# Moving the 72-row loads of strided values forward on the load queue, in a fused sparse attention and feed-forward kernel

## The chip, the cores and the metric

The kernel runs on one core of a Trainium2 chip. The metric is the device time of one execution in microseconds (us). Before the change the median of three runs is 280.25 us (278.87 to 281.23).

## What is computed

Attention over 8 batches, 8 heads, 576 positions and a head size of 64 is followed by a product of four weight matrices. Heads 0 to 3 see a local window of 32 positions; heads 4 to 7 see the positions that are congruent to their own modulo 32 ("strided").

```python
mask_local = (rel >= 0) & (rel < 32)
mask_strided = (rel >= 0) & (pos[None, :] % 32 == pos[:, None] % 32)
attn = softmax(where(mask, q @ k.T / 8, -1e9))
x = (attn @ v).transpose(0, 2, 1, 3).reshape(4608, 512)
out = (((x @ w1) * (x @ w2)) @ w3) @ w_out
```

w1 and w2 are 512 x 1024, w3 is 1024 x 1024 and w_out is 1024 x 512. Inputs and output are float32.

## The kernel before, in words

**Stages.** The program is one long unrolled order of work. TensorE's order is written out by hand (`pe` keeps it as written); the other engines follow it. Batch 0's attention runs alone at the start, four pairs of heads p0 to p3 (p0 and p1 local, p2 and p3 strided). Then come the first products of x with w1 and w2 (`aps` L535, `bps` L544), then eight rounds that fold w3 and w_out into one matrix w34 (`fold_tr` transposes a block of w3, L627; `fold_mm` multiplies it, L585). Batch 1's attention is spread among these rounds and the first outputs by the list `plan`. From then on each token tile's products (L535, L544, L585) host the next batch's attention in their gaps.

**Loads.** All loads are issued by one queue, SP (SyncE), in the order in which the program names them. A load writes float32 into a tile of the pool `stgp` (nine buffers), and an engine, mostly POOL (GpSimd), casts it to float16. An issue on SP waits until its buffer is free. It also waits on one of eight semaphores that the loads use in turn: a load waits until the load eight places ahead of it has landed.

The calls that set the order of the loads, in batch 0 and for the weights and batch 1, are:

```python
    load_qk(0, 0, "pa")
    load_rest(0, "v")
    load_qk(0, 1)
    load_vL(0)
    load_vX(0)
    load_w12(0)
...
    for jc in range(1, 6):
        load_w3(jc, "p")
    load_qk(1, 0)
    load_w3(6, "p")
    load_rest(1)
    load_w3(7, "p")
    load_vL(1)
    load_qk(1, 1)
    load_vX(1)
```

`load_qk` is a pair of loads of q and k for four heads (L182). `load_rest` loads their last 64 positions (L192). `load_vL` (L198) brings the values of the local heads: four transfers of 96 rows (L204), with a POOL cast (L205) and a POOL copy (L88) for each two heads. `load_vX` (L208) brings the values of the strided heads: four transfers of 72 rows into `sy` (L213), two of 7 rows (L218) and four of 112 rows (L220) into `st`, then a cast of `sy` (L221) and one or two casts of `st` (L223) on POOL, all into `v16X`. `load_w12` brings w1 and w2 (L173), `load_w3` (L162) and `load_wo` (L157) the other weights.

**Who waits for them.** The local pairs multiply by `v16L` and the strided pairs by `v16X` (`ah_PV`, L468). The first product with w1, `aps` at L535, needs the first cast of w1 into `w1h`. `fold_tr` of block jc needs the cast of that block of w3.

Of the kernel before, what the change touches and what calls it, by code (L numbers as in the profile page):

```python
# [14 lines left out]
def _ap(t: bass.AP, off_add, dims):  # L15
    return bass.AP(tensor=t.tensor, offset=t.offset + off_add, ap=dims)
# [3 lines left out]
def kernel(  # L20
# [11 lines left out]
    nc = tc.nc  # L32
    B, H, S, D = q.shape
# [15 lines left out]
    XW, XN, YW = 126, 4, 72  # L49
# [19 lines left out]
    AHEAD = 2  # L69
# [7 lines left out]
    def behind(ins):  # L77
        return tc.issue_after(ins.ins) if ins is not None else nullcontext()
# [4 lines left out]
    def copy(eng, out, in_):  # L83
        if eng == "a":
            return nc.scalar.copy(out=out, in_=in_)  # L85
        elif eng == "v":
            return nc.vector.tensor_copy(out=out, in_=in_)  # L87
        return nc.gpsimd.tensor_copy(out=out, in_=in_)  # L88
# [23 lines left out]
    for i in range(1, LT):  # L112
# [5 lines left out]
                          in_=_ap(maskX, 0, [[maskX.ap[0][0], XW], [0, XN - 1], [1, XW]]))  # L118
# [7 lines left out]
    v16X = [consts.tile([XW, 4, XN + 1, D + 1], FP16, name=f"v16X{i}") for i in range(2)]  # L126
# [33 lines left out]
    def load_w3(jc, eng):  # L160
        st = stgp.tile([P, DF], FP32, tag="stg")
        nc.sync.dma_start(st, moe_w3[bass.ds(jc * P, P), :])  # L162
        t = ffn.tile([P, DF], FP16, tag="w3n", bufs=6)
        w3n[jc] = t
        copy(eng, t, st)
# [13 lines left out]
    def load_qk(b, grp, engs="pp"):  # L179
        for nm, ten, eng in (("q", q, engs[0]), ("k", k, engs[1])):  # L180
            st = stgp.tile([P, 4, 4, D], FP32, tag="stg")
            nc.sync.dma_start(st.rearrange("p h c d -> p h (c d)"),  # L182
                              ten[b, 4 * grp:4 * grp + 4, 0:NM].rearrange("h (p c) d -> p h (c d)", c=4))
            t = qkp.tile([P, 4, 4, D], FP16, tag=f"{nm}{grp}")
            with behind(setup["p"] if b == 0 and grp == 0 else None):
                copy(eng, t, st.rearrange("p h c d -> p c h d"))
            x16[(b, nm, grp)] = t

    def load_rest(b, eng="p"):
        st = stgp.tile([P, H, D], FP32, tag="stg")  # L190
        for i, ten in enumerate((q, k)):
            nc.sync.dma_start(st[64 * i:64 * i + 64], ten[b, :, NM:S].rearrange("h p d -> p h d"))  # L192
        t = qkp.tile([P, H, D], FP16, tag="r")
        with behind(setup["v"] if b == 0 else None):
            copy(eng, t, st)
        x16[(b, "r")] = t

    def load_vL(b, hps=(0, 1)):  # L198
        vt = v16L[b % 2]
        for hp in hps:  # L200
            hs = slice(2 * hp, 2 * hp + 2)
            st = stgp.tile([P, 2, LT, D], FP32, tag="stg")
            for h in range(2):
                nc.sync.dma_start(st[0:LQ, h], v[b, 2 * hp + h].rearrange("(t p) d -> p t d", p=LQ))  # L204
            nc.gpsimd.tensor_copy(out=vt[0:LQ, hs, :, 0:D], in_=st[0:LQ])  # L205
            copy("p", vt[LQ:P, hs, 0:LT - 1, 0:D], vt[0:32, hs, 1:LT, 0:D])

    def load_vX(b):  # L208
        vt = v16X[b % 2]
        sv = v[b, 4:8]  # L210
        sy = stgp.tile([YW, 4, D], FP32, tag="stg")
        for h in range(4):
            nc.sync.dma_start(sy[:, h], sv[h].rearrange("(t x) d -> t x d", x=32)[:, 28:32])  # L213
        st = stgp.tile([XW, 4, 4 * D], FP32, tag="stg")
        n0 = 16 * 7
        for t in range(2):
            r0 = n0 + 7 * t
            nc.sync.dma_start(st[r0:r0 + 7], sv[:, NM + 32 * t:NM + 32 * t + 28].rearrange("h (a c) d -> a h (c d)", c=4))  # L218
        for h in range(4):
            nc.sync.dma_start(st[0:n0, h], sv[h, 0:NM].rearrange("(t a c) d -> t a (c d)", a=8, c=4)[:, 0:7])  # L220
        nc.gpsimd.tensor_copy(out=vt[0:YW, :, XN, 0:D], in_=sy)  # L221
        for hs in ((slice(0, 2), slice(2, 4)) if b == 0 else (slice(0, 4),)):
            nc.gpsimd.tensor_copy(out=vt[:, hs, 0:XN, 0:D], in_=st[:, hs].rearrange("p h (c d) -> p h c d", c=4))  # L223


# [511 lines left out]
    for p, s in enumerate(pairs):  # L737
        b, i = divmod(p, 4)
# [33 lines left out]
    load_qk(0, 0, "pa")  # L772
    load_rest(0, "v")
    load_qk(0, 1)
    load_vL(0)
    load_vX(0)
    load_w12(0)
    load_w12(1)
# [3 lines left out]
    for jc in range(1, 6):  # L782
        load_w3(jc, "p")
    load_qk(1, 0)
    load_w3(6, "p")
    load_rest(1)
    load_w3(7, "p")
# [4 lines that stand above are left out]
    while pos[0] < batch_end[0]:  # L792
# [28 lines left out]
    load_vL(2)  # L821
    load_qk(2, 1)
    load_vX(2)
    over = over_parts()
    tile1 = ab_parts(1) + o_parts(1)
# [66 lines left out]
```

## Time and profile before

| | before |
|---|---|
| median of three runs | 280.25 us |
| profiled execution | 278.93 us |
| its span | 277.2 us |
| TensorE busy | 259.6 us |
| POOL busy | 98.6 us |
| mean granted TensorE clock | 0.98 |
| bytes moved by the loads' queue | 38.87 MB |

Times in the profile count from the start of the span. PE is TensorE's matmul, PEld its weight load, DVE is VectorE, ACT ScalarE, POOL GpSimd, SP SyncE; SPq is SP's own queue, whose rows are issues of transfers. A row of the timeline has the start, the length, the engine, the line, the operation, its tiles, the number of instructions merged in it, and in brackets the idle time ahead of it with what ended it. A row of the windows view has a stretch, its length, the busy time of PE, PEld, DVE, ACT and POOL (with instructions), the granted TensorE clock, the mean busy share of the 16 DMA engines and the GB/s that they moved. Shares can pass 1, since packets overlap.

### The profile page before, as it was taken

To read this page: it belongs to the slowest core of one execution; us is meant where nothing else is said; L and a number is where in the kernel's file an instruction comes from. 1 tells how busy PE (TensorE), PEld (TensorE's weight loads), DVE (VectorE), ACT (ScalarE), POOL (GpSimd) and SP (SyncE) were. 2 spreads that over 40 slices of the span, in tenths; PEclk is the share of its full clock that TensorE was granted. 3 is DMA by queue.
4 is the path that set the end of the run, shared out by engine and by line. 5 is a ranking of instruction groups with operands and counts; after the bars stand their busy time and mean duration, and the time that the engine had idled before them with its cause. 6 is when DMAs were issued, how large, how long until landed. Compare 5 with 4: busy or idle time off the path is not lost.

```text
span 277.2 us, 6384 instructions
## 1 busy us (share of the span) xinstructions
PE 259.6 (94%) x2474; PEld 138.8 (50%) x2474; DVE 146.6 (53%) x334; ACT 146.7 (53%) x310; POOL 98.6 (36%) x116
## 2 busy tenths in 40 slices
PE   2956999989989999999999999999999999999995
PEld 1743345645645555555555555555555544444442
DVE  6551343346777547854875577467547752320320
ACT  2750433475755665666665655665665664324322
POOL 3545677493554813646637258200000000000000
PEclk9975999999999999999999999999999999999999
DMA  7949999958979759969699598410030003003003
GB/s 210 223 145 365 398 399 371 193 176 244 252 229 254 199 180 258 225 187 322 197 248 277 168 255 204 148 73 4 0 116 38 2 38 116 0 6 146 1 10 142
DMA packets 61310, 48.65 MB, mean 176 GB/s; under 512 B 32032, under 2 KB 52704, under 8 KB 61280
## 3 DMA queue, kind: packets, MB, share of 16 engines
q1 hardware_dynamic: 56096, 38.87, 50.7%
q10 hardware_dynamic: 5184, 9.37, 8.9%
q8 instruction: 19, 0.31, 0.5%
q14 instruction: 11, 0.09, 0.1%
HBM read 38.80 MB, written 9.44 MB: 174 GB/s over the span
## 4 chain that ended last, share of the span: by engine, by line
PE 87%; ACT 4%; DMA 3%; DVE 2%; issue 1%; SPq 1%; POOL 0%; DVEq 0%; ACTq 0%
PE ops L585 25%; PE aps L535 23%; PE bps L544 22%; PE sps L335 3%; PE ps L487 3%; PE sps L301 2%; PE pt L258 2%; DMA st<-in_k_dram 2%; DMA st<-in_moe_w_dram 2%; PE tps L345 1%; PE trp L627 1%; PE pt L301 1%; PE sps L415 1%; ACT ptm L440 1%; ACT pte L453 1%
## 5 line engine op out<-in xcount | busy, mean ns | idle before, releaser
L535 PE MATMUL aps<-xT,w1h 128*128 128x512 f16 (+1 forms) x288 | 75.3, 383 | 3.9 <-POOL w1h L88 3.4
L544 PE MATMUL bps<-xT,w2h 128*128 128x512 f16 (+1 forms) x288 | 74.7, 376 | 0.0
L585 PE MATMUL ops<-w,abt 128*128 128x512 f16 x280 | 67.0, 379 | 0.2 <-ACT osb L596 0.2
L547 DVE TENSOR_TENSOR abt<-bps,asb 128x512 f16<-128x512 f32 (+1 forms) x72 | 48.7, 679 | 32.2 <-PE bps L544 29.8
L515 ACT COPY asb<-aps 128x512 f32<-128x512 f32 (+1 forms) x72 | 42.4, 593 | 43.1 <-PE aps L535 39.2
L88 POOL CAST t<-st 128x1024 f16<-128x1024 f32 (+1 forms) x46 | 46.6, 1018 | 28.0 <-DMA st<-in_q_dram 13.4
L535 PEld LDWEIGHTS <-w1h 128*128 128x128 f16 x288 | 26.7, 99 | 33.9 <-POOL w1h L88 3.6
L544 PEld LDWEIGHTS <-w2h 128*128 128x128 f16 x288 | 26.1, 98 | 26.4 <-issue 0.3
L585 PEld LDWEIGHTS <-abt 128*128 128x128 f16 x280 | 25.3, 98 | 26.2 <-issue 0.3
L326 ACT ACTIVATE pte<-sps 128x1024 f16<-128x1024 f32 (+1 forms) x24 | 24.6, 1026 | 11.4 <-PE sps L301 11.4
L596 ACT COPY osb<-ops 128x512 f32<-128x512 f32 x35 | 20.6, 589 | 17.4 <-PE ops L585 17.4
L495 ACT COPY xT<-ps 128x504 f16<-128x504 f16 x16 | 9.2, 578 | 27.0 <-PE ps L487 27.0
L479 DVE TENSOR_TENSOR xqs<-sps,rcp 128x768 f16<-128x768 f32 (+1 forms) x24 | 21.4, 891 | 0.8
L315 DVE TENSOR_TENSOR ptm<-pte,maskL 128x1152 f16<-128x1152 f16 (+2 forms) x16 | 12.6, 790 | 15.1 <-ACT pte L326 13.6
L315 DVE TENSOR_TENSOR ptm<-pte,maskX 126x1152 f16<-126x1152 f16 (+2 forms) x16 | 12.0, 754 | 15.5 <-ACT pte L326 13.4
L85 ACT COPY qT<-pt 128x224 f16<-128x224 f16 (+4 forms) x60 | 18.0, 361 | 3.1 <-ACT osb L596 1.9
L223 POOL CAST v16X<-st 126x1024 f16<-126x1024 f32 (+1 forms) x9 | 8.8, 975 | 28.8 <-DMA st<-in_v_dram 26.4
L205 POOL CAST v16L<-st 96x768 f16<-96x768 f32 x16 | 14.4, 899 | 8.3 <-DMA st<-in_v_dram 5.8
L585 PE MATMUL ops<-woh,w3T 128*128 128x512 f16 x64 | 15.6, 379 | 0.0
L487 PEld LDWEIGHTS <-xqs 126*128 126x128 f16 (+3 forms) x176 | 12.0, 100 | 7.2 <-DVE xqs L479 0.6
L87 DVE COPY kT<-pt 128x512 f16<-128x512 f16 (+4 forms) x48 | 14.1, 323 | 1.2 <-ACT qT L85 0.5
L487 PE MATMUL ps<-id,xqs 126*128 126x126 f16 (+3 forms) x176 | 14.4, 215 | 0.2 <-DVE xqs L479 0.2
(95 smaller groups left out, 248.3 us busy)
## 6 DMA issues: line engine op xcount, KB each, us to landing
out_dram<-osb ACTq DMA_DIRECT2D x35, 256.0 KB
st<-in_q_dram SPq DMA_DIRECT2D x16, 512.0 KB
st<-in_k_dram SPq DMA_DIRECT2D x16, 512.0 KB
st<-in_moe_w_dram SPq DMA_DIRECT2D x16, 512.0 KB
st<-in_v_dram SPq DMA_DIRECT2D x32, 144.0 KB
st<-in_v_dram SPq DMA_DIRECT2D x32, 112.0 KB
st<-in_moe_w_out_dram SPq DMA_DIRECT2D x4, 512.0 KB
st<-in_q_dram SPq DMA_DIRECT2D x8, 128.0 KB
```

What stands on the lines that cost most here:

```text
L85: return nc.scalar.copy(out=out, in_=in_)
L88: return nc.gpsimd.tensor_copy(out=out, in_=in_)
L315: nc.vector.tensor_mul(o.rearrange("p (a x) -> p a x", x=x), i.rearrange("p (a x) -> p a x", x=x), _ap(s.mask, lo, [[s.mask.ap[0][0], s.kr ...
L326: nc.scalar.activation(out=pv[0:kr, :, lo:hi], in_=src, func=AF.Exp, bias=0.0, scale=scale)
L479: nc.vector.tensor_mul(s.xqs[0:w, c0:c0 + l].rearrange("p i h d -> p h i d"), xv[:, :, :, 0:D], _ap(rcp, 0, [[rcp.ap[0][0], w], [LT, 2], [ ...
L487: pe(nc.tensor.transpose(ps[:, s.q[t]:s.q[t] + l], s.xqs[0:l, t].rearrange("p h d -> p (h d)"), id16[0:l, 0:l]))
L515: nc.scalar.copy(out=st["asb"][:, 0:nt], in_=st["a"][:, 0:nt])
L535: pe(nc.tensor.matmul(st["a"][:, 0:nt], w1h[:, ci, bass.ds(jc * P, P)], xT[ci][:, tok], start=(ci == 0), stop=(ci == KM - 1)))
L544: pe(nc.tensor.matmul(st["b"][:, 0:nt], w2h[:, ci, bass.ds(jc * P, P)], xT[ci][:, tok], start=(ci == 0), stop=(ci == KM - 1)))
L547: nc.vector.tensor_mul(abts[tch][:, jc, skip:], st["b"][:, 0:nt], st["asb"][:, 0:nt])
L585: pe(nc.tensor.matmul(st["ps"], lhs(ci), rhs(ci), start=(ci == 0), stop=(ci == KF - 1)))
L596: nc.scalar.copy(out=osb, in_=ps)
```

## The change

The four 72-row transfers and the cast of `sy` become a function of their own, `load_vX0`. For batch 0 it is called ahead of `load_vL(0)`, for batch 1 between `load_qk(1, 0)` and `load_w3(6)`. For the later batches `load_vX` calls it at its start, where the transfers stood. The cast of `st` is split in two for batch 1 as well as for batch 0. In the order of the built program the 182 instructions of SP are the same ones; POOL has one more; on DVE a reciprocal and a multiplication of pair p2 change places. The orders on PE and ACT are unchanged. Line numbers after the function grow by 5 (L218 and L220 by 6), and L213 becomes L212.

```diff
-    def load_vX(b):
-        vt = v16X[b % 2]
+    def load_vX0(b):
         sv = v[b, 4:8]
         sy = stgp.tile([YW, 4, D], FP32, tag="stg")
         for h in range(4):
             nc.sync.dma_start(sy[:, h], sv[h].rearrange("(t x) d -> t x d", x=32)[:, 28:32])
+        nc.gpsimd.tensor_copy(out=v16X[b % 2][0:YW, :, XN, 0:D], in_=sy)
+
+    def load_vX(b):
+        vt = v16X[b % 2]
+        sv = v[b, 4:8]
+        if b >= AHEAD:
+            load_vX0(b)
         st = stgp.tile([XW, 4, 4 * D], FP32, tag="stg")
...
-        nc.gpsimd.tensor_copy(out=vt[0:YW, :, XN, 0:D], in_=sy)
-        for hs in ((slice(0, 2), slice(2, 4)) if b == 0 else (slice(0, 4),)):
+        for hs in ((slice(0, 2), slice(2, 4)) if b < AHEAD else (slice(0, 4),)):
             nc.gpsimd.tensor_copy(out=vt[:, hs, 0:XN, 0:D], in_=st[:, hs].rearrange("p h (c d) -> p h c d", c=4))
...
     load_qk(0, 1)
+    load_vX0(0)
     load_vL(0)
     load_vX(0)
     load_w12(0)
...
     load_qk(1, 0)
+    load_vX0(1)
     load_w3(6, "p")
     load_rest(1)
     load_w3(7, "p")
```

AHEAD is 2.

## The prediction

> **What bounds the kernel now.** I read the page first (busy shares, the slices, the chain), then the chain in order of time, then the timelines of PE, SP and POOL over the first 24 us, then the windows.
>
> ```profile
> PEclk9975999999999999999999999999999999999999
> DMA  7949999958979759969699598410030003003003
> ...
> PE 87%; ACT 4%; DMA 3%; DVE 2%; issue 1%; SPq 1%; POOL 0%; DVEq 0%; ACTq 0%
> ```
>
> PE carries 87% of the chain, so only its holes can be shortened by moving loads. Nearly all the hole time lies in the first 24 us, where slices 3 and 4 also show a granted clock of 0.7 and 0.5. Slice 3 (13.9 to 20.8 us) has the DMA engines at 4 tenths, between fuller slices: something other than the DMA engines holds the loads there.
>
> The chain in order of time, and PE's own rows at that place:
>
> ```profile
> 17.55 4.77 DMA st<-in_moe_w_dram
> ...
> 22.37 1.05 POOL w1h L88
> ...
> 23.47 1.03 PE aps L535 x2
> ```
>
> ```profile
> 15.94 0.54 PE L468 MATMUL xpl<-v16L,ptm 128*128 128x65 f16 x12
> ...
> 18.82 0.76 PE L468 MATMUL xpl<-v16X,ptm 126*128 126x65 f16 x10 [2.08 <-POOL v16X L223]
> 19.39 0.68 PE L487 MATMUL ps<-id,xqs 128*128 128x128 f16 x6
> 23.47 1.03 PE L535 MATMUL aps<-xT,w1h 128*128 128x512 f16 x2 [3.40 <-POOL w1h L88]
> ```
>
> PE idles 2.08 us for the strided values and 3.40 us for the first cast of w1. From 23.47 on it is nearly full. The end is therefore set by when w1's first load is issued (17.55), and that by SP, whose rows follow end to end:
>
> ```profile
> 4.87 4.78 SPq L204 DMA_DIRECT2D st<-in_v_dram  x4
> 9.69 3.41 SPq L213 DMA_DIRECT2D sy<-in_v_dram  x4
> 13.14 0.81 SPq L218 DMA_DIRECT2D st<-in_v_dram  x2
> 14.00 3.43 SPq L220 DMA_DIRECT2D st<-in_v_dram  x4
> 17.55 4.66 SPq L173 DMA_DIRECT2D st<-in_moe_w_dram  x8
> ```
>
> ```profile
> 4.90:9.70 4.80, 3.77 (x30) 2.61 (x32) 3.02 (x10) 2.32 (x4) 1.50 (x2) 1.00 1.15 313
> 9.70:12.30 2.60, 2.59 (x43) 2.04 (x40) 0.91 (x4) 2.27 (x6) 1.74 (x3) 1.00 1.28 220
> 12.30:17.50 5.20, 4.11 (x71) 3.18 (x68) 3.55 (x12) 4.12 (x9) 3.19 (x5) 1.00 0.24 68
> 17.50:20.50 3.00, 1.25 (x16) 1.05 (x15) 1.25 (x5) 0.52 (x2) 1.23 (x2) 0.53 0.63 201
> 20.50:24.00 3.50, 0.53 (x2) 0.26 (x3) 0.13 (x1) 0.25 (x1) 1.39 (x2) 0.50 1.00 359
> 24.00:28.00 4.00, 4.00 (x23) 1.99 (x22) 1.33 (x5) 0.58 (x1) 2.77 (x3) 0.51 1.00 369
> ```
>
> The DMA engines are full to 12.3 us, at a share of 0.24 and 68 GB/s from 12.3 to 17.5, and full again from 20.5. In the middle stretch SP's issuing is the bound.
>
> The Trainium skill (DMA: Bandwidth & Descriptors, section Issuing engines are not separate DMA queues) says that the time to start a transfer is usually small beside the transfer. Here the trace differs: 0.24. By that rule the order of issue would be worth nothing and the sum would stay 280.25, which is the first rival's result.
>
> **The change, part by part.**
>
> *Batch 0, the 72-row transfers go ahead of the 96-row ones.* SP issues the same 18 transfers of q's rest to w1, so the question is whether the order changes what they cost. Single issues from the timeline of SP:
>
> ```profile
> 6.06 0.63 SPq L204 DMA_DIRECT2D st<-in_v_dram  x1
> ...
> 7.77 1.88 SPq L204 DMA_DIRECT2D st<-in_v_dram  x1
> ...
> 14.68 1.47 SPq L220 DMA_DIRECT2D st<-in_v_dram  x1
> ...
> 16.82 0.60 SPq L220 DMA_DIRECT2D st<-in_v_dram  x1
> ```
>
> A 96-row issue takes 0.63 us or 1.88 us; the long one falls while the DMA engines still drain q and k, so I read its excess of 1.25 us as SP held by a full queue. The small issues at 9.69 (0.85 each) bring little data, and are sent when the queue is about to run empty. After the change the four small ones are sent in the full stretch: 4.87 + 3.41 = 8.28. Then come the four 96-row ones. By the rule of the eight semaphores the third and the fourth wait for q's and k's second loads to land, which the casts show:
>
> ```profile
> 9.08 1.04 POOL L88 CAST t<-st 128x1024 f16<-128x1024 f32 x1 [3.30 <-DMA st<-in_q_dram]
> 10.63 1.04 POOL L88 CAST t<-st 128x1024 f16<-128x1024 f32 x1 [0.51 <-DMA st<-in_k_dram]
> 12.02 0.83 POOL L205 CAST v16L<-st 96x768 f16<-96x768 f32 x1 [0.35 <-DMA st<-in_v_dram]
> 12.91 0.71 POOL L88 COPY v16L<-v16L 32x640 f16<-32x640 f16 x1
> ...
> 15.35 0.40 POOL L221 CAST v16X<-sy 72x256 f16<-72x256 f32 x1
> 18.16 0.61 POOL L223 CAST v16X<-st 126x512 f16<-126x512 f32 x1 [2.41 <-issue]
> 19.46 0.62 POOL L223 CAST v16X<-st 126x512 f16<-126x512 f32 x1 [0.70 <-DMA st<-in_v_dram]
> ```
>
> So the fourth can't go before 10.6 us. It then takes 0.63 at least (11.25, against 13.14 before for the next issue: 1.9 us earlier) and 1.88 at most (12.5: 0.6 us earlier). If the excess returns in full and the first three also take their old times, nothing is gained; if the long 112-row issue (1.47, 0.87 over its neighbours) no longer meets what held it, 0.9 more is gained. Bounds: 0 and 2.8 us. I take 1.9, the row of 0.63 for the fourth, since the two loads ahead of it that filled the queue have landed by then.
>
> The 96-row loads are issued up to 3.41 us later. Their data lands when the DMA engines reach it, and these are full until 12.3 in either order, so the first cast (12.02) moves by about 0.5 us, bounded by 0 and 3.4. The product of p1 (15.94) then slips by as much. What hides it is PE's idle 2.08 + 3.40 = 5.5 us, more than the upper bound, so this costs 0. Without that cover it would cost the 0.5. The cast of sy (0.40) moves to an idle place of POOL (between 11.7 and 12.0). The casts of st (18.16, 19.46) and w1's first load (17.55) come 1.9 us earlier; with the first cast of w1, PE resumes at 21.6 instead of 23.47. What is late next there is still w1: the strided product and transposition, 1.25 us of PE work, end near 18.2. The swapped reciprocal on DVE lies in the same hole: 0.
>
> *Does the 1.9 us last?* Every later weight load follows w1's in one full queue (DMA share 1.00 from 20.5 on), so casts and PE move together. The narrowest place is the transposition of w3's block 1, then block 6:
>
> ```profile
> 40.80 1.04 POOL L88 CAST t<-st 128x1024 f16<-128x1024 f32 x1 [0.22 <-DMA st<-in_moe_w_dram]
> ...
> 51.58 1.04 POOL L88 CAST t<-st 128x1024 f16<-128x1024 f32 x1 [1.22 <-DMA st<-in_moe_w_dram]
> ...
> 65.70 1.05 POOL L223 CAST v16X<-st 126x1024 f16<-126x1024 f32 x1 [3.35 <-DMA st<-in_v_dram]
> ```
>
> ```profile
> 42.60 0.61 PE L627 MATMUL trp<-id,t 128*128 128x128 f16 x8
> ...
> 53.92 0.61 PE L627 MATMUL trp<-id,t 128*128 128x128 f16 x8
> ...
> 72.03 0.28 PE L468 MATMUL xps<-v16X,ptm 126*128 126x65 f16 x4 [0.18 <-ACT pte L453]
> ```
>
> Block 1 has 42.60 - 41.84 = 0.76 us to spare, block 6 has 53.92 - 52.62 = 1.30 us.
>
> *Batch 1, the same transfers go ahead of w3's block 6.*
>
> ```profile
> 39.55 2.60 SPq L162 DMA_DIRECT2D st<-in_moe_w_dram  x1
> ...
> 55.67 3.32 SPq L213 DMA_DIRECT2D sy<-in_v_dram  x4
> ```
>
> Four issues of 3.32 us enter the queue ahead of block 6's issue at 39.55, past the rest of q and k, block 7, batch 1's local values and the last q and k. Block 6 is issued at 39.55 and its cast starts at 51.58, 12 us later: that is the depth of the queue, and its issue of 2.60 us is again SP held back. So I let 3.32 us of issuing be covered by the 2.60 us and the depth, and charge only the data: 4 x 72 rows x 256 bytes = 74 KB, 0.3 us at the 220 GB/s of the window 9.70:12.30. The bounds are 0.3 and 3.32 + 0.40 (the cast of sy at 15.35) = 3.7. With 0.3, block 6 keeps 1.0 us to spare: cost 0. The strided values of batch 1 gain nothing: their cast ends at 66.75 and PE wants them at 72.03, after ACT. Splitting that cast (1.05 into 2 x 0.61, 0.17 more on POOL) is hidden by the same 5 us. Batch 2's loads, queued behind, come earlier, and no row of the chain waits for them.
>
> *Sum.* On the profiled execution: 278.93 - 1.9 = 277.0 us (span 277.2 to 275.3). The median shown is 1.32 above that execution; on its scale 280.25 - 1.9 = 278.35, say 278.4 us.
>
> **The rivals.**
>
> *Nothing moves.* The 4.78 and 3.41 us are the transfers' own costs in any order: w1 is still issued at 17.55. For it: the bound 0 above. Against it: 0.63 beside 1.88 for the same shape. 280.2 us.
>
> *The clock comes back sooner.* PE runs at a granted 0.50 to 0.53 from 17.5 to 28.0, as the windows show, so the 4.5 us of work from 23.47 to 28 could be done in half. If PE's hole shrinks (the 2.08 us goes, and w1 comes by 2.8 us earlier), the clock may not fall, or may return one period earlier: about 2.2 us more, 278.4 - 2.2 = 276.2 us. For it: the hole is just 3.40 us. Against it: strided values and w1 move together, so the hole keeps its length. The Trainium skill (TensorE: Matmul & The Clock Gate, Part 1) has the clock halve after an idle window of about 3.4 us and return after a busy one, the windows running freely; by that rule a slightly shorter hole gives this rival's time, and the phase alone scatters runs.
>
> *Block 6 comes late (the slower side).* If the queue ahead of block 6 runs dry during the four issues, its cast is later by the full 3.7 us. It decides from 1.30 us on: PE then stands for 3.7 - 1.3 = 2.4 us, the gain of 1.9 is gone, and 0.5 is lost: 280.8 us; 282.7 if batch 0 gave nothing either. For it: POOL does wait 1.22 us for block 6. Against it: 12 us between issue and cast.
>
> **How the numbers follow.** Forecast 0.50 (277.4 to 279.7 by its own terms, gains of 2.8 and 0.6), nothing moves 0.20, clock 0.16, block 6 late 0.14. The range 275.8 to 281.3 leaves out the far ends of the last two and some of the scatter of 2.4 us between the three runs. One per cent, 2.8 us, is about what a measurement of this kernel can tell from no change. Faster by over 1% means under 277.45: most of the clock case and a tenth of the forecast, 0.20. Slower by over 1% means over 283.05: the far end of the block 6 case with the scatter, 0.08. The rest, 0.72, is within 1%.
>
> **What would show it.** Right: SP's four 96-row issues start near 8.3 and together take under 3.5 us, the first w1 issue stands near 15.6, `aps` L535 starts near 21.6, and L627 shows no idle time ahead of its sixth and seventh blocks. Wrong: w1's issue still near 17.5 (nothing moves), a granted clock of 1.0 before 25 us (clock), or PE idle on a w3 cast near 52 us (block 6).

## The result, and the profile after

The changed kernel takes 278.07 us (median of 9 runs, 277.18 to 281.36) against 280.17 us for the kernel before, run beside it (9 runs, 278.87 to 281.67): a ratio of 0.9921, 95% interval 0.9892 to 0.9951. Measured once more it was 277.44 against 279.32 us, 0.9933 (0.9909 to 0.9957). The ratios leave out single runs more than 1.5% above the fastest of the same kernel, here the one of 281.36 us. So it is about 2 us faster, which is inside 1%. The profiled execution took 277.72 us with a span of 276.0 us, 1.2 us under that of before.

From the page after, the granted clock and the DMA engines in 40 slices, and the chain by engine:

```profile
PEclk9999999999999999999999999999999999999999
DMA  7979999999749659759699796510030012003013
PE 78%; DMA 11%; DVE 3%; ACT 3%; SPq 2%; issue 1%; POOL 1%; POOLq 0%
```

Slice 3 of the DMA engines has risen from 4 to 7 tenths, the clock does not fall in this execution, and DMA has gone from 3% of the chain to 11%. SP's own rows show where the time was won:

```profile
4.88 3.41 SPq L212 DMA_DIRECT2D sy<-in_v_dram  x4
8.33 2.75 SPq L204 DMA_DIRECT2D st<-in_v_dram  x4
11.12 0.75 SPq L224 DMA_DIRECT2D st<-in_v_dram  x2
11.91 2.54 SPq L226 DMA_DIRECT2D st<-in_v_dram  x4
14.57 6.84 SPq L173 DMA_DIRECT2D st<-in_moe_w_dram  x8
```

The four 72-row issues cost 3.41 us, as before. The 96-row ones fell from 4.78 to 2.75 us (0.87 us of which is a wait ahead of the fourth, until k's second load has landed), the 112-row ones from 3.43 to 2.54 us. Thus w1's first load is issued at 14.57 us instead of 17.55. The windows view of the same stretches:

```profile
12.30:17.50 5.20, 4.86 (x91) 3.97 (x90) 2.76 (x11) 3.72 (x8) 3.67 (x5) 1.00 0.70 190
20.50:24.00 3.50, 3.04 (x28) 1.58 (x26) 1.34 (x5) 0.91 (x2) 1.84 (x2) 1.00 0.96 325
28.00:40.00 12.00, 9.78 (x54) 4.42 (x53) 5.06 (x9) 4.00 (x7) 9.32 (x10) 1.00 1.05 400
```

The DMA share from 12.3 to 17.5 us is 0.70 instead of 0.24, and TensorE keeps its full clock. But from 28 to 40 us PE is busy for 9.78 us of 12 only, beside DMA engines that are full. Its timeline, POOL's, and the chain tell why:

```profile
18.01 0.36 PE L473 MATMUL xpl<-v16X,ptm 126*128 126x65 f16 x6 [0.31 <-DVE xqs L484]
19.82 0.60 PE L540 MATMUL aps<-xT,w1h 128*128 128x512 f16 x2 [0.93 <-POOL w1h L88]
...
39.76 0.62 PE L632 MATMUL trp<-id,t 128*128 128x128 f16 x8 [1.83 <-POOL t L88]
...
51.09 0.61 PE L632 MATMUL trp<-id,t 128*128 128x128 f16 x8
...
61.81 0.35 PE L473 MATMUL xps<-v16L,ptm 128*128 128x65 f16 x6 [0.50 <-DVE xqs L484]
```

```profile
18.73 1.04 POOL L88 CAST w1h<-st 128x1024 f16<-128x1024 f32 x1 [0.49 <-DMA st<-in_moe_w_dram]
...
38.67 1.04 POOL L88 CAST t<-st 128x1024 f16<-128x1024 f32 x1
...
49.78 1.04 POOL L88 CAST t<-st 128x1024 f16<-128x1024 f32 x1 [0.94 <-DMA st<-in_moe_w_dram]
```

```profile
18.22 9.63 DMA st<-in_moe_w_dram
27.92 10.70 DMA st<-in_moe_w_dram
```

The holes of 2.08 and 3.40 us have shrunk to 0.31 and 0.93 us. `aps` starts 3.65 us earlier (23.47 to 19.82). Then PE stands for 1.83 us at w3's block 1, whose cast came only 2.13 us earlier (40.80 to 38.67); the chain shows the loads unbroken from 18.2 to 38.6 us. Block 1's transposition starts 2.84 us earlier (42.60 to 39.76): the stream's 2.13 us and the 0.76 us that the block had to spare before, less 0.05. Block 6 is cast 1.80 us earlier and ready at 50.82, with 0.27 us to spare.

Of the 2.84 us just 2.06 are left from the PE row at 61.81 us on, to PE's end. The stream has no part in that loss. PE waits there for DVE, whose mask multiplications of batch 1 run beside casts of POOL:

```profile
58.99 1.32 DVE L320 TENSOR_TENSOR ptm<-pte,maskL 128x640 f16<-128x640 f16 x1
```

```profile
57.61 2.35 POOL L88 CAST t<-st 128x1024 f16<-128x1024 f32 x2
59.98 1.55 POOL L228 CAST v16X<-st 126x512 f16<-126x512 f32 x2
```

The same multiplication took 0.49 us in the kernel before (at 61.59), where the cast of batch 1's strided values came later (65.70). That 2.06 us is near the stream's 2.13 is chance, then: in the second execution of the changed kernel this place costs 0.05 us.

### The profile page after: what moved, and what is told of

Read it like the earlier page. It is cut to its first block, busy times and chain, and to the rows that moved or that the text cites. A ratio compares the mean times of both kernels' runs of the same rounds, so it can differ in the third digit from the quotient of the medians.

```text
span 276.0 us, 6387 instructions
## 1 busy us (share of the span) xinstructions
PE 258.3 (94%) x2474; PEld 137.8 (50%) x2474; DVE 147.3 (53%) x334; ACT 146.9 (53%) x310; POOL 97.4 (35%) x117
## 4 chain that ended last, share of the span: by engine, by line
PE 78%; DMA 11%; DVE 3%; ACT 3%; SPq 2%; issue 1%; POOL 1%; POOLq 0%
PE ops L590 24%; PE aps L540 20%; PE bps L549 19%; DMA st<-in_moe_w_dram 7%; PE sps L340 3%; PE ps L492 3%; DMA st<-in_k_dram 2%; PE sps L306 2%; PE pt L263 2%; DVE ptm L320 2%; DMA st<-in_v_dram 1%; PE pt L306 1%; PE trp L632 1%; ACT qT L85 1%; SPq L226 1%
## 5 line engine op out<-in xcount | busy, mean ns | idle before, releaser
L540 PE MATMUL aps<-xT,w1h 128*128 128x512 f16 (+1 forms) x288 | 73.6, 377 | 1.8 <-POOL w1h L88 0.9
L88 POOL CAST t<-st 128x1024 f16<-128x1024 f32 (+1 forms) x46 | 45.0, 983 | 32.3 <-DMA st<-in_k_dram 13.5
L590 PE MATMUL ops<-woh,w3T 128*128 128x512 f16 x64 | 15.6, 379 | 0.0
L340 PEld LDWEIGHTS <-ptm 128*128 128x128 f16 (+1 forms) x264 | 11.2, 97 | 6.0 <-DVE ptm L320 0.8
```

The source lines that it names most:

```text
L540: pe(nc.tensor.matmul(st["a"][:, 0:nt], w1h[:, ci, bass.ds(jc * P, P)], xT[ci][:, tok], start=(ci == 0), stop=(ci == KM - 1)))
L590: pe(nc.tensor.matmul(st["ps"], lhs(ci), rhs(ci), start=(ci == 0), stop=(ci == KF - 1)))
```

## The experiments

The theory after the result: loads issued without a break feed one stream (w1, w2, w3, w_out, in this order), and its lead, not PE's lead or the clock, is what reaches the end. It held in part only, as told below the table. Each kernel is timed beside runs of the kernel before on the same chip. "PE end" is the end of PE's last matmul in the profiled execution, "clock" the granted clock from 20.5 to 24.0 us.

| kernel | first w1 issue | `aps` starts | clock | block 1 cast | block 1 transposed | PE end | ratio to before |
|---|---|---|---|---|---|---|---|
| before | 17.55 | 23.47 | 0.50 | 40.80 | 42.60 | 273.78 | 1 |
| changed | 14.57 | 19.82 | 1.00 | 38.67 | 39.76, waits 1.83 | 271.67 | 0.9921 (0.9892 to 0.9951) |
| batch 0 only | 14.42 | 19.91 | 1.00 | 39.23 | 40.33, waits 1.68 | 272.79 | 0.9975 (0.9949 to 1.0000) |
| batch 1 only | 17.11 | 22.52 | 0.51 | 39.49 | 41.73 | 274.00 | 1.0006 (0.9992 to 1.0019) |
| ACT's queue | 15.08 | 21.93 | 1.00 | 40.00 | 41.10, waits 1.63 | 272.37 | 0.9939 (0.9925 to 0.9954) |
| before, kept warm | 17.11 | 23.16 | 1.00 | 40.17 | 41.27, waits 0.56 | 274.09 | 1.0031 (1.0009 to 1.0054) |
| changed, again | 14.48 | 20.70 | 0.52 | 38.34 | 39.61 | 270.79 | 0.9933 (0.9909 to 0.9957) |
| block 1 ahead | 14.49 | 20.41 | 0.52 | 36.33 | 39.44 | 272.05 | 0.9953 (0.9935 to 0.9972) |
| and `sy` behind | 14.53 | 19.71 | 1.00 | 35.78 | 37.64 | 271.90 | 0.9948 (0.9926 to 0.9971) |
| two w1 ahead | 10.98 | 20.81 | 0.67 | 36.96 | 39.13 | 271.08 | 0.9913 (0.9882 to 0.9944) |
| one w1 ahead | 11.09 | 19.76 | 0.56 | 37.88 | 38.98, waits 0.29 | 271.69 | 0.9914 (0.9878 to 0.9949) |

One execution differs from the next: "batch 1 only" is the kernel before up to 38 us, yet has `aps` 0.95 us earlier. Less than 1 us between the PE ends of two kernels is therefore not taken for a difference between them.

Two things come out of the columns. At block 1 PE's lead over the kernel before is the smaller of two: the lead that PE brings, and the lead of block 1's cast plus the 0.76 us which block 1 had to spare before. In the five kernels that wait there, the cast's lead plus 0.76 gives 2.89, 2.33, 1.56, 1.39 and 3.68 us (changed, batch 0 only, ACT's queue, kept warm, one w1 ahead), and PE's lead measures 2.84, 2.27, 1.50, 1.33 and 3.62. Where there is no wait, PE's own lead passes block 1 whole: 2.99 us in "changed, again", 3.47 in "two w1 ahead". And behind block 1 a lead can still be lost: in the kernels that leave the order w1, w2, w3, w_out as it was, between nothing ("changed, again") and 1.64 us ("kept warm") up to PE's end.

**Batch 0's part alone, batch 1's part alone.** In `load_vX` the condition `b >= AHEAD` becomes `b`, batch 1's cast of `st` is in one piece again, and one call goes:

```diff
-    load_vX0(1)
     load_w3(6, "p")
```

> Only the move in batch 0; batch 1's 72-row transfers and its undivided cast stay where they were before the change. Theory (batch 0 carries the whole gain, because SP's issues overlap the full DMA queue): the first w1 issue stands near 14.6 us as in the changed kernel, and the time is 277.7 to 278.6 us, a ratio of 0.991 to 0.995 to before. Rival (batch 1 carries part of it): 279 us or more, a ratio of 0.996 or above.

For the other half the condition becomes `b != 1` and `load_vX0(0)` goes:

```diff
-    load_vX0(0)
     load_vL(0)
```

> Only the move in batch 1, with the cast of its 112-row tile in two. Theory: no row of the chain waits for it, the queue ahead of w3's block 6 hides the four issues: 279.7 to 280.7 us, a ratio of 0.998 to 1.002. Rival (block 6 comes late): 281 us or more. Rival (batch 1 carries part of the gain): 279.3 us or less.

Batch 1's part alone is worth nothing (1.0006). Batch 0's alone gives 278.13 against 279.2 us, 0.9975. The time lies in the expected range, but the kernel before was faster here too, and the ratio lies in the rival's: the earlier w1 issue and the wait at block 1 are there, and half the gain is missing. Its PE is level with the changed kernel's at 62 us (61.73 and 61.81) and 0.97 us behind it at 92 us, one step of it here (PE, then DVE, then POOL of "batch 0 only"):

```profile
85.31 0.54 PE L340 MATMUL sps<-v16L,ptm 128*128 128x65 f16 x12 [0.22 <-DVE ptm L320]
```

```profile
83.75 1.51 DVE L320 TENSOR_TENSOR ptm<-pte,maskL 128x1152 f16<-128x1152 f16 x1 [0.89 <-ACT pte L331]
```

```profile
83.60 1.05 POOL L228 CAST v16X<-st 126x1024 f16<-126x1024 f32 x1 [2.54 <-DMA st<-in_v_dram]
```

The mask multiplication takes 1.51 us where a cast of POOL runs beside it; the shortest ones take 0.76 us. This became a question of its own, below.

**The 72-row issues on ACT's queue.** In the changed kernel, batch 0's four transfers are issued by ACT at the very start, and the cast is held behind k's:

```diff
-    load_vX0(0)
+    sy_cast = load_vX0(0, nc.scalar)
     load_qk(0, 0, "pa")
...
+    with behind(setup["qk"]):
+        sy_cast()
     load_vL(0)
```

> The changed kernel with batch 0's four 72-row transfers issued from ACT's queue at the start, ahead of its table load, so that SP issues 3.4 us less. Theory (a full queue holds SP, so the four 96-row issues grow again to 4 us or more when they follow q and k directly): the first w1 issue moves from 14.57 to 13.3 to 14.0 us, and the time is 277.0 to 277.8 us. Rival (an issue has a fixed cost, whatever stands in the queue): the first w1 issue near 11.2 us and a time of 276.5 us or less. Rival (the stream of weights is bound elsewhere): w1 earlier and the time unchanged, 278.1.

With four issues of 0.85 us fewer, SP reaches w1 not earlier but at 15.08 us, where 13.3 to 14.0 was expected. SP's rows, and what it waited for up to 16 us:

```profile
7.51 4.06 SPq L204 DMA_DIRECT2D st<-in_v_dram  x4
...
15.08 2.41 SPq L173 DMA_DIRECT2D st<-in_moe_w_dram  x4
```

```profile
SPq L204 <- DMA sy<-in_v_dram: 2.4, 2, 1.9
SPq L182 <- DMA sy<-in_v_dram: 1.3, 1, 1.3
```

Most of what was saved went into waits: by the rule of the eight semaphores, q's second load and the first two 96-row loads now wait for the 72-row transfers to land, 3.7 us in all. The last of the 96-row issues, ahead of which there is no wait, takes 2.08 us here and 0.31 us in the changed kernel:

```profile
9.49 2.08 SPq L204 DMA_DIRECT2D st<-in_v_dram  x1
```

```profile
10.76 0.31 SPq L204 DMA_DIRECT2D st<-in_v_dram  x1
```

So the time of an issue isn't fixed by its shape: that reading of the prediction's 1.88 us row is shown, and the rival of a fixed cost falls. That a full queue holds SP is a name for it which no row shows directly. The times of the four together (4.78, 2.75 and 4.06 us in three orders) aren't a clean measure of it, since 0.87 us of the 2.75 and 0.53 of the 4.06 are waits for a landing. The kernel's time, 0.9939, can't be told from the changed kernel's.

**The kernel before, kept warm.** 30 and 54 matmuls of no use fill the two holes, so that the clock doesn't fall:

```diff
+    def keep(n):
+        ps = psF.tile([P, 2 * NM], FP16, tag="f", name="kps")
+        warm(ps, n)
...
+    add(keep, 30)
...
+    add(keep, 54)
```

> The kernel before, with 30 and 54 matmuls of 128 columns whose result nobody reads in the two holes of PE (ahead of the product of p2, and ahead of the first product with w1), so that its clock does not fall; the loads are untouched. Theory (the clock alone is worth only what w3's block 1 has to spare, 0.76 us, since the stream of weights sets that place): 279.2 to 280.2 us, the granted clock 1.0 throughout, and idle time of PE ahead of the transposition of block 1. Rival (the kept clock is the gain): 278.0 to 278.4 us, as in the changed kernel.

The clock is 1.00, PE leads the kernel before by 2.23 us at 25.3 us, and the time is 0.3% longer. The timeline of PE and the cast it waits for:

```profile
23.16 0.61 PE L535 MATMUL aps<-xT,w1h 128*128 128x512 f16 x2 [0.36 <-POOL w1h L88]
...
41.27 0.62 PE L627 MATMUL trp<-id,t 128*128 128x128 f16 x8 [0.56 <-POOL t L88]
```

```profile
40.17 1.04 POOL L88 CAST t<-st 128x1024 f16<-128x1024 f32 x1 [0.24 <-DMA st<-in_moe_w_dram]
```

PE runs into block 1 and is left with 1.33 us of lead, of which 0.63 come from this execution's earlier stream (40.80 to 40.17). The wait at block 1 ends the rest of the 2.23 us. What PE has left there is lost behind block 1, in steps at which PE waits for DVE: 0.22 us remain at 87 us. Two mask multiplications on the way (at 79 and 85 us) take 1.24 and 1.44 us, the shortest 0.76. Of the 1.1 us by which the profiled span is longer, 0.81 lie behind PE's end, in the wait for the output (last section). So keeping the clock did not give the gain, and the rival falls; that the stream alone cancelled it is not shown.

**The changed kernel again.** No edit.

> The changed kernel once more, beside the two kernels below on one chip. Theory (the gain is the 2 us by which the stream of weight loads starts earlier, given as PE's lead from 61.8 us on): the ratio to the kernel before lies at 0.9925, between 0.990 and 0.995, and PE again waits about 1.8 us for the cast of w3's block 1 near 39.8 us. Rival (part of the 0.0079 was luck of the phase between POOL's casts and DVE's mask multiplications, since the kernel with batch 0's part alone measured 0.9975): the ratio comes out at 0.995 to 0.998.

The gain held. This execution was profiled with a fallen clock, which makes it the counterpart of the last experiment. The window from 20.5 to 24.0 us and PE's rows:

```profile
20.50:24.00 3.50, 3.30 (x19) 1.63 (x20) 1.15 (x4) 0.00 (x0) 2.36 (x4) 0.52 0.99 348
```

```profile
20.70 1.04 PE L540 MATMUL aps<-xT,w1h 128*128 128x512 f16 x2 [2.54 <-POOL w1h L88]
...
39.61 0.61 PE L632 MATMUL trp<-id,t 128*128 128x128 f16 x8
```

w1's first cast came 0.87 us later, the hole grew from 0.93 to 2.54 us, and PE ran at half speed. It still reached block 1 at 39.61 us, without a wait, where the execution at full clock stood from 37.93 to 39.76. The expected wait of 1.8 us did not show: such a wait only gives back the time that a full clock has won. PE's lead at block 1, 2.99 us, is its own and more than the stream's 2.46, and it is still 2.99 us at PE's end. By the Trainium skill (TensorE: Matmul & The Clock Gate, Part 1) the gate's window of about 3.4 us runs freely, so the same kernel meets it in another phase each time. The two executions can't show the phase, since their holes differ too: a clock of 1.00 behind 0.93 us of idle, of 0.52 behind 2.54 us. The second hole is shorter than that window, and the clock fell all the same.

**Block 1 of w3 ahead of half of w_out; then `sy` of batch 1 behind block 7 as well.**

```diff
     load_w3(0, "p")
-    for g in range(4):
-        load_wo(g, "p")
-    for jc in range(1, 6):
+    load_wo(0, "p")
+    load_wo(1, "p")
+    load_w3(1, "p")
+    load_wo(2, "p")
+    load_wo(3, "p")
+    for jc in range(2, 6):
         load_w3(jc, "p")
```

> The changed kernel with the load of w3's block 1 moved ahead of the second half of w_out (same bytes, same issues, another order). Theory (the stream of weight loads, not the clock, ended the lead that PE had): PE is free at 37.93 us and finds block 1 cast, so the wait of 1.83 us ahead of its transposition goes; the second half of the block-0 product then waits for the last w_out cast (39.7 us), about 0.9 us in two places; PE leads the changed kernel by about 0.9 us at 41 us. At block 6, whose cast ends at 50.8 us as before, 0.3 us of it is left: 0.3 us faster than the changed kernel at the end. Rival (the lead was lost to something else, the wait at block 1 being only where it shows): PE is no earlier at 41 us, and the end is within 0.2 us of the changed kernel or later.

```diff
-    load_vX0(1)
     load_w3(6, "p")
     load_rest(1)
     load_w3(7, "p")
+    load_vX0(1)
```

> As the kernel above, and batch 1's four 72-row transfers with their cast moved from ahead of w3's block 6 to behind block 7. Theory: those transfers held block 6's cast back by about 1.3 us in the changed kernel (POOL waits 0.94 us for it); without them it ends near 49.5 us, all of the 0.9 us survives blocks 6 and 7, and the kernel is 0.9 us faster than the changed kernel, ratio to before near 0.989. Rival (the 72-row transfers ahead of block 6 cost nothing there, as the prediction had it): the same time as the kernel above, 0.3 us or less faster than the changed kernel. The strided values of batch 1 arrive later than in the changed kernel, but not later than in the kernel before, where PE had over 5 us to spare for them.

Both missed: neither is faster than the changed kernel (0.9953 and 0.9948). The first was profiled with a fallen clock and had no wait to save. It led the kernel before by 3.16 us at block 1 and lost 0.53 us at block 6, where PE stood for 0.36 us, and 0.73 us near 62 us, at the place where the changed kernel lost its 0.66 in one step. The second kept its clock, and shows what the order inside the stream is worth (PE's timeline):

```profile
37.64 0.61 PE L632 MATMUL trp<-id,t 128*128 128x128 f16 x8
39.32 0.59 PE L590 MATMUL ops<-woh,w3T 128*128 128x512 f16 x2 [1.07 <-POOL woh L88]
40.66 0.59 PE L590 MATMUL ops<-woh,w3T 128*128 128x512 f16 x2 [0.75 <-POOL woh L88]
```

The wait is gone from block 1 and stands, 1.07 + 0.75 = 1.82 us of it, at the two halves of w_out that now come last. Nor did `sy` hold block 6 back by 1.3 us: with `sy` behind, PE still waits 0.32 us for block 6. From block 1's cast to block 6's the changed kernel takes 11.11 us, and 10.83 in its second execution; "batch 0 only", without `sy` between, takes 10.87. The 0.3 us which the prediction charged can't be told from this scatter.

**Without POOL's later casts.** To see what batch 1's part is worth when DVE meets no cast, three kernels (before, changed, batch 0 only) leave out POOL's casts of batches 2 to 7, for instance:

```diff
+            if b >= AHEAD:
+                x16[(b, nm, grp)] = x16[(1, nm, grp)]
+                continue
             t = qkp.tile([P, 4, 4, D], FP16, tag=f"{nm}{grp}")
```

> The kernel before without POOL's casts of batches 2 to 7: their loads are still issued and land, but attention of these batches works on batch 0's and 1's cast tiles (leaves out those casts, so its output holds other values). Meant to be compared with the next two, which leave out the same. Theory (a mask multiplication on DVE takes 0.76 us alone and up to 1.5 us beside a POOL cast, and PE waits behind it): all 24 multiplications take 0.76 to 0.80 us, and the kernel is 0.2 to 0.8 us faster than with the casts. Rival (their length has another cause, such as loads landing in memory): some still take over 1.1 us.

> The changed kernel without POOL's casts of batches 2 to 7 (left out as in the kernel above). Theory: 2.1 us less than the kernel above in the trace, set at block 1 of w3 and batch 1 and kept to the end, since no later multiplication is lengthened. Rival (batch 1's part has a worth of its own): 2.1 us less as well, but 0.8 us less than the next kernel.

> The kernel with batch 0's part alone, without POOL's casts of batches 2 to 7 (left out as in the two above). Theory (what it lacked against the changed kernel, 0.8 us in the span, was lost where DVE's mask multiplications met casts of later batches, a matter of phase): within 0.3 us of the changed kernel without the casts, and 1.8 to 2.1 us under the kernel before without them. Rival (batch 1's part itself brings the 0.8 us): 0.8 us slower than the changed kernel without the casts.

The groups of the local mask multiplications, of "batch 0 only" and then of the same without the casts:

```profile
L320 DVE TENSOR_TENSOR ptm<-pte,maskL 128x1152 f16<-128x1152 f16 x12 | 11.3, 943 | 13.6 <-ACT pte L331 13.6
```

```profile
L331 DVE TENSOR_TENSOR ptm<-pte,maskL 128x1152 f16<-128x1152 f16 x12 | 9.1, 758 | 13.6 <-ACT pte L342 13.6
```

All 24 of batches 2 to 7 (local and strided) now take 0.76 us in all three kernels, so POOL's casts are the cause of the longer ones: shown. The Trainium skill (GPSIMD Engine Reference, section 1, Specifications) says that POOL's way into on-chip memory is shared with VectorE and contended when a VectorE instruction has two inputs there. This multiplication reads `pte` and `maskL`, and the trace agrees: 0.76 us alone, up to 1.57 us beside a cast in "batch 0 only". The excess over 24 times 0.76 us was 1.45 us in the kernel before, 1.08 in the changed one, 4.41 in "batch 0 only". Batch 1's eight narrower multiplications are not in these sums; the casts of batches 0 and 1 stay in all kernels.

Medians without the casts are 278.96 (before), 276.79 (changed, 2.17 us less) and 277.33 us (batch 0 only), ratios to the full kernel before 0.9985 (0.9963 to 1.0007), 0.9906 (0.9872 to 0.9940) and 0.9917 (0.9888 to 0.9945). The kernel before gains 0.43 us by it (279.39 to 278.96), as expected, though the interval covers no change. PE ends at 274.81, 272.14 and 272.48 us. The last two lie 0.34 us apart, where with the casts it was 1.12 us. So most of what "batch 0 only" lacked in its profile was lost where multiplications met casts. The lead at block 1 over the kernel before without the casts (its block 1 is transposed from 43.29 us) is 2.61 us for the changed kernel and 2.46 for "batch 0 only"; at PE's end it is 2.67 and 2.33. Without the later casts it reaches the end nearly whole. In the medians "batch 0 only" is 1.63 us under the kernel before, short of the expected 1.8 to 2.1, and 0.54 us above the changed kernel, with intervals that overlap. Whether batch 1's part has a worth of its own of up to about half a microsecond stays open.

**w1 ahead of the remaining strided values.** If only the stream's start counts, the DMA share of 0.70 ahead of it can still be filled:

```diff
+    load_w12(0, 0, 2)
     load_vX(0)
-    load_w12(0)
+    load_w12(0, 2, 4)
```

> The changed kernel with the first two loads of w1 (and their casts) ahead of batch 0's remaining strided values. Theory (PE is paced from 20 to 52 us by when the stream of weight loads delivers, so only an earlier stream counts, and the DMA engines' share of 0.70 between 12.3 and 17.5 us leaves 0.3 x 5.2 = 1.5 us of transfer time to fill): w1's first issue near 11.1 us instead of 14.57, the DMA share near 1.0 in that stretch, the cast of w3's block 1 1.0 to 1.5 us earlier than in the changed kernel; the strided values are cast near 19.5 us, so PE waits about 2 us for them instead of 0.3 and 0.9 us, which costs nothing. End 1.0 to 1.5 us earlier: ratio to before 0.988 to 0.990. Rival (the order of the loads counts, whichever PE wants first should come first): the 1.7 us later strided values are paid in full, slower than the changed kernel, ratio 0.995 or above.

The other kernel has 1 in the place of both 2s.

> The same with only the first load of w1 ahead of the remaining strided values. Theory: half the dose. One load of 0.5 MB takes 1.4 us of the DMA engines, which is all that stands idle there, so nearly the same gain: 0.7 to 1.4 us under the changed kernel, ratio to before 0.988 to 0.991, with a shorter wait for the strided values. Rival: between the changed kernel and the kernel above, which it has slower, ratio about 0.994.

The windows view of the first, its PE, and its cast of block 1:

```profile
12.30:17.50 5.20, 3.80 (x68) 3.04 (x66) 3.55 (x12) 4.02 (x9) 4.12 (x5) 1.00 1.03 281
```

```profile
19.76 0.76 PE L475 MATMUL xpl<-v16X,ptm 126*128 126x65 f16 x10 [3.25 <-POOL v16X L230]
...
39.13 0.61 PE L634 MATMUL trp<-id,t 128*128 128x128 f16 x8
```

```profile
36.96 1.04 POOL L88 CAST t<-st 128x1024 f16<-128x1024 f32 x1 [0.23 <-DMA st<-in_moe_w_dram]
```

The share is 1.03, block 1 is cast 1.71 us earlier than in the changed kernel, and a wait of 3.25 us for the strided values costs nothing against it. So the order rival falls. But the expected 1.0 to 1.5 us didn't come: 276.66 against 279.84 us, 0.9913, whose interval covers the changed kernel's ratios. Block 1 is ready at 38.00 us and PE gets to it at 39.13: the bound has moved from the stream to PE, which has lost its clock (0.67) in that hole. The kernel with one load has the same in small (0.9914). These are the lowest ratios of full kernels here, but no gain over the changed kernel is shown: PE of the kernel with one load ends at 271.69 us, as the changed kernel's does at 271.67, and its span is shorter by the last wait alone (last section).

## Why the prediction was right, and where its steps were not

- **What bounds the kernel**: right up to 23 us. SP's issuing held w1 back, and the earlier issue carried the gain.
- **The order of the issues**: right in kind, mis-sized. The predicted w1 issue was 15.6 us, the measured one 14.57; the gain was 2.98 us, not 1.9, just over the upper bound of 2.8. The fourth 96-row issue went at 10.76, as the sum had it (not before 10.6), and took 0.31 us and not 0.63; the long 112-row issue lost its excess too (3.43 to 2.54), which I had put at the bound and not in the sum.
- **Local values later, at no cost**: right. The first cast moved from 12.02 to 12.28 us, and PE has no wait there. The product of p1 slipped by 0.80 us (15.94 to 16.74), inside the cover.
- **"Strided values and w1 move together, so the hole keeps its length"**: wrong. The hole shrank to 0.93 us in one execution and to 2.54 in the next, and in the profiled one the clock stayed at 1.00 before 25 us, which I had named as a sign of being wrong. But the clock rival's price was wrong as well: PE's lead grew from 3.65 us at `aps` to 5.57 at full clock, and block 1 left 2.84 of it.
- **"Casts and PE move together"**: the step that failed. The stream's lead was 2.13 us, less than the 2.98 us of the issue, and PE's was 2.84 us behind block 1: more than the stream's, as it used up the 0.76 us that I had named as spare. Block 6 kept 0.27 us. "No idle ahead of the sixth and seventh blocks" held.
- **Behind block 1**: the sum had no term for what comes later. In the profiled execution 0.66 us went in one step at 61.81 us, where DVE's multiplications meet casts, and in the second one next to nothing.
- **Batch 1**: the time agrees with cost 0 and gain 0 (1.0006 alone). The 0.3 us of data isn't resolved. That nothing of batch 1's part costs time is not shown: in the profiled execution its moved cast lies beside the multiplications at 60 us.
- **Sum**: 278.4 us forecast, 278.07 measured, and the closeness is in part luck. The term of 1.9 us was too small: the lead at block 1 was 2.84 and 2.99 us in the two executions. What took the surplus away stood nowhere in the sum: the loss behind block 1 in one of them, and a wait at the kernel's end that was longer by 0.93 and 0.77 us (last section), so that the spans fell by 1.2 and 2.2 us. The median fell by 2.10 us, in the repetition by 1.88.

## What to carry to other kernels

When loads come as one stream that is full, ask of any earlier start which of two things moved: the stream, or the engine that eats it. At each tile the engine keeps the smaller of its own lead and the stream's lead plus the slack that the tile had; an order inside the stream, or a faster clock, can just move the wait. What is kept can still be lost further on, here where another engine's work met casts, so follow the lead row by row to the end before putting a gain down to one cause. The time of an issue can depend on its place (0.31 to 2.08 us for one shape here), and a load that is issued early can make later ones wait for its landing: look at both before moving transfers.

## Unexpected in the hardware

The time between PE's end and the end of the span is no constant: 3.41 us before, 4.34 us after, 3.1 to 4.3 us over all kernels. It is the last wait for the write of the output. SP's waits at the end, after and then before:

```profile
SPq L894 <- DMA out_dram<-olast: 2.4, 1, 2.4
```

```profile
SPq L887 <- DMA out_dram<-olast: 1.2, 1, 1.2
```

The bytes are the same. In the execution of after, the last 4.6 us also hold a packet of a queue that carries instructions, which the end of before lacks (DMA view, with packets, MB and share):

```profile
q14 instruction: 1, 0.01, 0.5%
```

The fourteen profiles fall into two groups by this. Nine have such a packet between PE's end and the end of the span, 1.1 to 1.6 us behind PE's end; there SP's last wait is 2.0 to 2.4 us and the whole stretch 3.9 to 4.3. The five others (before, "batch 1 only", before without POOL's casts, and the two with w1 ahead) have none, a wait of 1.2 us and a stretch of 3.1 to 3.4. Both profiles of the changed kernel are among the nine, so up to 0.9 us of what it gains may be lost here, and the kernels with w1 ahead owe a part of their low ratios to it. Whether the packet delays the write wasn't tried; it stays open, as does what happens in the runs that were not profiled.
